# A second level of the seven-product scheme for three of 28 products per unit, with reordered copies, one buffer less for q, and a changed first unit and end

## The chip, the core and the metric

The kernel runs on one core of a Trainium2 chip. The metric is the device time of one execution in microseconds. A core has TensorE (PE, matrix products; its weight loads are listed apart as PEld), VectorE (DVE), ScalarE (ACT), GpSimd (POOL) and SyncE (SP, which here only issues DMAs). TensorE writes its results to PSUM, which has eight banks of 512 fp32 values per partition; the other engines' working memory is SBUF.

## What is computed

Attention over pooled keys and values, then a two-layer network with a sine in it. All numbers are fp32; q, k and v are 8 x 8 x 576 x 64 (batch, heads, sequence, head size), w_in is 512 x 2048, w_out is 2048 x 512.

```python
k_p = k.reshape(B, H, Sp, 8, D).mean(axis=3)          # Sp = 72
v_p = v.reshape(B, H, Sp, 8, D).mean(axis=3)
scores = scale * np.matmul(q, k_p.transpose(0, 1, 3, 2))
scores = scores - np.max(scores, axis=-1, keepdims=True)
attn = np.exp(scores)
attn = attn / (np.sum(attn, axis=-1, keepdims=True) + 1e-09)
x = np.matmul(attn, v_p)     # then heads are joined: 4608 tokens x 512
h = x @ w_in
s = np.sin(alpha * h)
g = h + s * s / (alpha + 1e-09)
out = g @ w_out
```

## The kernel before

**Two stages.** The first stage makes x batch by batch and g from it, and stores g to HBM ("g_bridge"). The second stage loads g and multiplies it by w_out. Line L796 is every matmul of x by w_in, L1133 every matmul of g by w_out.

**Seven products instead of eight.** Both stages use the scheme in which the product of two 2 x 2 block matrices takes seven block products, with sums of blocks made before and sums of products made after. In the first stage a block product is 256 features by 256 inputs by 256 tokens: two feature blocks and two input blocks of 128, so four matmuls with 256 moving columns. The sums of the weights are the tiles as1, as2, as4 (and a21, which is overwritten by a difference), the sums of x are in bt (tile "home3"). The second stage has applied the scheme twice all along (`outer` and `inner`), down to matmuls with 144 columns.

**Units, groups, slots.** The first stage runs over nine units of 512 tokens (`hidden(u, extra)`). A unit has four groups J of 2 x 256 features, and a group has seven slots k, one block product each, in the order 1, 5, 6, 2, 7, 3, 4. Slot numbers run from 0 to 27 within a unit, so that the third group (J = 2) begins at slot 14 and the fourth at slot 21. The whole program order on each engine is written out by hand. Before each slot's product, the list `self.left` of the slot before runs (the work on ScalarE and VectorE that belongs to the group: left0 to left6), then the list `extra[slot]`.

**Sums of products in PSUM.** The seven products accumulate in four banks, b1, b6, b5 and b7, taken in turn from banks 0 to 4. Product 1 goes to b1, and ScalarE copies b1 to b6; product 6 is added to b6, and ScalarE copies b6 to b7; product 5 goes to b5 and is copied to the SBUF tile p5. Products 2, 7, 3 and 4 are added to b1, b7, b6 and b7. The copies are L822 (b1 to b6), L836 (b6 to b7) and L838 (p5); VectorE's adds of p5 are L775. The sine is L802, the square L809, `finish` (L867) adds the squares to h, and `store_g` (L874) issues two DMAs from SP. h and g share the tile "h", which has two buffers.

**Attention in between.** While unit u runs, the attention of batch b = u + 1 is computed by `extra` work, placed by `carry(u)`: two_scores (L302) and its maxima and differences (two_shifts: L325, L326), exp (L351), norm (L357 to L359), turn (transposes on VectorE, L485 to L495), move (16 DMAs from SP, L505, tr to aM), all_values (L594 and L607 on TensorE, L521 to x on ScalarE). In all_values a copy of one column, named "order" (L601), stands between two parts of the matmuls into one bank. turn_q (L215, L218) transposes q of a later batch on VectorE, and 16 DMAs (L228) put it into place. Batch 0 is handled by first_batch, before unit 0. q tiles come from a pool with two buffers of one name; load_q is L80 and L101. load_v and load_k are followed by pooling sums on POOL (L127).

**The second stage.** `outputs()` runs 8 batches x 7 outer products; each has seven inner products, four matmuls each. For one outer product st, product 1 goes first and is copied to a second bank (L1230), and later products 6 and 7 each need a copy (L1253, L1272); in between stand products 5, 4, 2 and 3 of the outer product before it (`last`). `combine` adds the result to output blocks, `out` transposes a block on VectorE (L1155) and issues four DMAs (L1160).

Of the kernel before, what the change touches and what calls it, by code (L numbers as in the profile page):

```python
# [13 lines left out]
F32 = mybir.dt.float32  # L14
# [5 lines left out]
P = 128  # L20
# [20 lines left out]
class Kernel:  # L41
# [33 lines left out]
    def new_q(self, b):  # L75
        self.qm[b] = self.qp.tile([P, 5 * self.H * self.D], F32, name="q")
# [6 lines left out]
    def pairs_q(self, b, tiles):  # L83

        nc = self.nc
        if 0 in tiles:
            self.raw = self.q_views(self.qm[b])
            self.qm[b] = self.qp.tile([P, 5 * self.H * self.D], F32, name="q")
# [113 lines left out]
    def turn_q(self, b, part):  # L202
# [8 lines left out]
        if part == 0:  # L211
            for e in range(2):
                x = main[:, 4 * e:4 * e + 4].rearrange("p hp t (k i) -> p hp t k i", i=32).rearrange("p hp t k i -> p (hp t) k i")
                out = tr[:, :, 768 * e:768 * e + 512].rearrange("p k (n i) -> p n k i", i=32)
                nc.vector.transpose(out=out, in_=x)  # L215
            return
# [26 lines left out]
    def attention(self, b):  # L243
# [22 lines left out]
        def q_t(i, copy=nc.scalar.copy):  # L266
# [3 lines left out]
            if b not in self.qt:  # L270
                self.qt[b] = self.qt_view(self.qp.tile([P, 5 * H * D], F32, name="q"))
# [105 lines left out]
        def q_head(hp):  # L377

            if hp == 0:
                self.qt[b] = self.qt_view(self.qp.tile([P, 5 * H * D], F32, name="q"))  # L380
# [203 lines left out]
        def all_values():  # L584
# [16 lines left out]
            (nc.vector.tensor_copy if b > 1 else nc.scalar.copy)(out=self.sm.tile([P, 1], F32, name="order")[:], in_=rest[:, 1, 0:1])  # L601
# [6 lines left out]
            self.vp.pop(b)  # L608
            for hp in hps:
                to_x(ps[hp].rearrange("p (t j) -> p j t", t=4), hp, 0, 512)  # L610
# [149 lines left out]

    def sums_of_x(self, u, n):
# [9 lines left out]
    def hidden(self, u, extra):  # L771

        nc = self.nc
        bank = lambda: self.bank([P, JW, TH])
        add = lambda o, x, y: nc.vector.tensor_tensor(out=o, in0=x, in1=y, op=OP.add)  # L775

        for slot in range(7 * self.NJ):
            J, k = divmod(slot, 7)
            for f in self.left:
                f()  # L780
            for f in extra[slot]:
                f()
            if k == 0:
                before = self.group
                G = self.group = SimpleNamespace(
                    u=u, J=J, b1=bank(), g=self.hp.tile([P, 2, JW, 2, TH], F32, name="h"),
                    s=self.hp.tile([P, 2, JW, 2, TH], F32, name="s", bufs=1))
            xT, bt = self.xT[u], self.bt[u]
            B = lambda i, j: xT[:, 2 * i:2 * i + 2, j * TH:(j + 1) * TH]

            def product(p, ps, start):
                x = {1: B(0, 0), 2: B(1, 0), 3: B(1, 1), 4: bt[:, 3], 5: bt[:, 0], 6: bt[:, 1], 7: bt[:, 2]}[p]
                for jj in range(JW):
                    f = J * JW + jj
                    for kk in range(2):
                        nc.tensor.matmul(ps[:, jj, :], self.A[p][:, kk, f * P:(f + 1) * P], x[:, kk, :],  # L796
                                         start=(start and jj == 0 and kk == 0), stop=(kk == 1), skip_group_check=True)

            def sin(G, i, j, src):
                for jj in range(JW):  # L800
                    f = i * self.K2 // 2 + G.J * JW + jj
                    nc.scalar.activation(out=G.s[:, i, jj, j, :], in_=src[:, jj], func=AF.Sin, scale=self.al[:, f:f + 1])  # L802

            def square(G, i, js):

                for jj in range(JW):
                    f = i * self.K2 // 2 + G.J * JW + jj
                    x = G.s[:, i, jj, js, :]
                    nc.scalar.activation(out=x, in_=x, func=AF.Square, scale=self.c[:, f:f + 1])  # L809

            early = lambda G: G.J == (0 if G.u else 1)

            def squares(G):
                if not early(G):
                    square(G, 0, 1)
                square(G, 1, slice(0, 2))

            self.squares = squares

# [566 lines left out]
```

## Time and profile before

| | |
|---|---|
| three timed runs | 909.52, 909.93, 910.46 us |
| the profiled execution, span | 906.9 us |
| TensorE clock granted | 1.00 throughout |
| units 1 to 6 | 55.4 us each |
| first stage ends, second begins to dominate | about 519 us |
| last matmul ends | 901.8 us |
| ScalarE busy from 140 to 500 us | 257.10 of 360 us |
| VectorE busy from 140 to 500 us | 226.01 of 360 us |
| POOL busy from 140 to 500 us | 91.64 of 360 us |
| DMA engines' share and rate, 140 to 500 us | 0.60, 176 GB/s |

How to read it: a span is the time from the first to the last instruction that the profiler recorded, somewhat less than the device time. A busy share is an average over stages with different limits. An fp32 matmul appears as two records, each with its own weight load; the duration of a record (381 ns for 256 columns) is its latency, and since matmuls are pipelined the step from one to the next is shorter. In the groups, "idle before, releaser" tells how long the engine stood idle just before and what ended the wait. In the chain of waits each line is start, duration and what the chain ran through.

### The profile page before, as it was taken

To read this page: it belongs to the slowest core of one execution; us is meant where nothing else is said; L and a number is where in the kernel's file an instruction comes from. 1 tells how busy PE (TensorE), PEld (TensorE's weight loads), DVE (VectorE), ACT (ScalarE), POOL (GpSimd) and SP (SyncE) were. 2 spreads that over 40 slices of the span, in tenths; PEclk is the share of its full clock that TensorE was granted. 3 is DMA by queue.
4 is the path that set the end of the run, shared out by engine and by line. 5 is a ranking of instruction groups with operands and counts; after the bars stand their busy time and mean duration, and the time that the engine had idled before them with its cause. 6 is when DMAs were issued, how large, how long until landed. Compare 5 with 4: busy or idle time off the path is not lost.

```text
span 906.9 us, 17532 instructions
## 1 busy us (share of the span) xinstructions
PE 898.2 (99%) x6906; PEld 813.9 (90%) x6906; DVE 664.9 (73%) x1000; ACT 436.2 (48%) x998; POOL 169.9 (19%) x159
## 2 busy tenths in 40 slices
PE   8999999999999999999999999999999999999997
PEld 5787888888888788888888999999999999999997
DVE  7685766758467584664557799979798888889895
ACT  5696775867668676686976621111111111111111
POOL 4685340804408043130000000000000000000000
PEclk9999999999999999999999999999999999999999
DMA  9985867759567575548217247161618162534401
GB/s 263 243 250 157 220 172 191 191 169 251 174 167 184 168 195 173 143 128 308 77 69 244 96 132 214 43 207 40 223 27 229 35 194 68 171 92 131 131 15 40
DMA packets 128746, 141.12 MB, mean 156 GB/s; under 512 B 46920, under 2 KB 95704, under 8 KB 128664
## 3 DMA queue, kind: packets, MB, share of 16 engines
q1 hardware_dynamic: 126312, 137.99, 53.0%
q10 hardware_dynamic: 2352, 2.01, 0.8%
q8 instruction: 55, 0.90, 0.4%
q14 instruction: 27, 0.22, 0.1%
HBM read 75.37 MB, written 47.19 MB: 135 GB/s over the span
## 4 chain that ended last, share of the span: by engine, by line
PE 97%; DVE 1%; DMA 1%; ACT 1%; issue 0%; SPq 0%; DVEq 0%; ACTq 0%
PE PS L796 48%; PE PS L1133 42%; PE PS L302 2%; PE PS L594 2%; PE PS L607 1%; DMA h<-in_k_dram 1%; PE PS L406 0%; DVE h L867 0%; PE PS L552 0%; PE PS L263 0%; ACT s L809 0%; PE PS L199 0%; PE PS L550 0%; PE PS L460 0%; DMA out_dram<-o 0%
## 5 line engine op out<-in xcount | busy, mean ns | idle before, releaser
L796 PE MATMUL PS<-home,a 128*128 128x256 f32 x1152 | 264.4, 381 | 1.0 <-ACT home L521 0.5
L796 PEld LDWEIGHTS PS<-home,a 128*128 128x128 f32 x1152 | 216.5, 190 | 37.4 <-issue 5.0
L796 PE MATMUL PS<-home,as 128*128 128x256 f32 x864 | 200.0, 380 | 0.0
L796 PEld LDWEIGHTS PS<-home,as 128*128 128x128 f32 x864 | 162.6, 190 | 23.0 <-issue 0.8
L1133 PE MATMUL PS<-s,wb 128*128 128x144 f32 x896 | 119.4, 286 | 0.4 <-ACT PS L1253 0.4
L1133 PEld LDWEIGHTS PS<-s,wb 128*128 128x128 f32 x896 | 113.7, 190 | 0.7 <-ACT PS L1253 0.6
L809 ACT ACTIVATE s<-s,c 128x256 f32<-128x256 f32 (+1 forms) x216 | 110.0, 572 | 0.0
L127 POOL TENSOR_TENSOR kvin<-kvin 96x768 f32<-96x768 f32 (+3 forms) x42 | 72.5, 1726 | 197.6 <-DMA kvin<-in_v_dram 196.0
L775 DVE TENSOR_TENSOR h<-PS,p 128x512 f32<-128x512 f32 x72 | 49.1, 684 | 77.4 <-PE PS L796 44.6
L802 ACT ACTIVATE s<-h,al 128x256 f32<-128x256 f32 x144 | 65.1, 503 | 54.4 <-DVE h L775 53.8
L1253 ACT COPY PS<-PS 128x144 f32<-128x144 f32 x56 | 14.7, 263 | 146.3 <-PE PS L1133 142.0
L802 ACT ACTIVATE s<-PS,al 128x256 f32<-128x256 f32 x144 | 60.0, 467 | 32.8 <-PE PS L796 17.0
L1133 PE MATMUL PS<-s,a 128*128 128x144 f32 x512 | 73.2, 286 | 0.0
L1133 PE MATMUL PS<-r,wb 128*128 128x144 f32 x512 | 73.2, 286 | 0.0
L867 DVE TENSOR_TENSOR h<-PS,s 128x512 f32<-128x512 f32 x36 | 24.6, 684 | 62.4 <-ACT s L809 62.4
L1133 PEld LDWEIGHTS PS<-r,wb 128*128 128x128 f32 x512 | 67.1, 190 | 0.1
L1133 PEld LDWEIGHTS PS<-s,a 128*128 128x128 f32 x512 | 67.0, 190 | 0.0
L1272 ACT COPY PS<-PS 128x144 f32<-128x144 f32 x56 | 14.7, 263 | 88.2 <-PE PS L1133 88.2
L1133 PE MATMUL PS<-x,wb 128*128 128x144 f32 x384 | 54.9, 286 | 0.0
L1133 PE MATMUL PS<-s,we 128*128 128x144 f32 x384 | 54.9, 286 | 0.0
L1133 PEld LDWEIGHTS PS<-s,we 128*128 128x128 f32 x384 | 50.3, 190 | 0.1
L1133 PEld LDWEIGHTS PS<-x,wb 128*128 128x128 f32 x384 | 50.3, 190 | 0.0
(188 smaller groups left out, 1185.8 us busy)
## 6 DMA issues: line engine op xcount, KB each, us to landing
g_bridge<-h SPq DMA_DIRECT2D x72, 512.0 KB
r<-g_bridge SPq DMA_DIRECT2D x31, 1152.0 KB
out_dram<-o SPq DMA_DIRECT2D x124, 72.0 KB
kvin<-in_k_dram SPq DMA_DIRECT2D x14, 576.0 KB
q<-in_q_dram SPq DMA_DIRECT2D x7, 1024.0 KB
kvin<-in_v_dram SPq DMA_DIRECT2D x14, 512.0 KB
aM<-tr SPq DMA_DIRECT2D x54, 92.0 KB
aM<-tr SPq DMA_DIRECT2D x54, 88.0 KB
```

Source lines behind the costliest of these rows:

```text
L127: self.nc.gpsimd.tensor_tensor(out=t[..., 0:w] if w > D else out, in0=t[..., 0:w], in1=t[..., w:2 * w], op=OP.add)
L302: nc.tensor.matmul(ps[e][r0 + r:r0 + r + q.shape[-1], h, :], q[s], kb[s, hp, :], start=True, stop=True)
L594: nc.tensor.matmul(o[r:r + 64], w, x, start=start and i < 2, stop=False, skip_group_check=True)
L607: nc.tensor.matmul(ps[hp], w.rearrange("p e d -> p (e d)"), x, start=False, stop=True, skip_group_check=True)
L775: add = lambda o, x, y: nc.vector.tensor_tensor(out=o, in0=x, in1=y, op=OP.add)
L796: nc.tensor.matmul(ps[:, jj, :], self.A[p][:, kk, f * P:(f + 1) * P], x[:, kk, :], start=(start and jj == 0 and kk == 0), stop=(kk == 1), ...
L802: nc.scalar.activation(out=G.s[:, i, jj, j, :], in_=src[:, jj], func=AF.Sin, scale=self.al[:, f:f + 1])
L809: nc.scalar.activation(out=x, in_=x, func=AF.Square, scale=self.c[:, f:f + 1])
L867: add = lambda o, x, y: self.nc.vector.tensor_tensor(out=o, in0=x, in1=y, op=OP.add)
L1133: nc.tensor.matmul(out, W[:, J // 2, J % 2, :], A[:, J, :], start=(start and J == 0), stop=(J == self.NJ - 1), skip_group_check=True)
L1253: nc.scalar.copy(out=x1[:, 0, :], in_=x0[:, 1, :])
L1272: nc.scalar.copy(out=x1[:, 1, :], in_=x1[:, 0, :])
```

## The change

**Second level.** In units 1 to 6, product 5 of the third group and products 5 and 1 of the fourth group are not computed with four matmuls of 256 columns, but with the seven-product scheme once more: seven matmuls of 128 x 128 x 128. `inner_w_in` makes four sums of the weights per product, once, on POOL (slot 23 of unit 0); `inner_x` makes four sums of x per product and unit on POOL (slot 2). `inner_product` has four pieces: a (two matmuls into a spare bank, 7 or 6, and two ScalarE copies), b (two matmuls and a copy within the bank), d (one matmul and an add on VectorE) and e (two matmuls). The pieces are spread between the halves of the other products.

**Order in the third and fourth group.** The copies of the third group stand ahead of the last sines of the second group on ScalarE, and products 4, 6, 7 and 3 there are split in two or more parts. A part of `finish` and the store of the third group's g come later, in slots 23 and 25; `store_g` then stands behind the 16 DMAs of turn_q on SP's queue. The fourth group's first sine stands behind the "order" copy, which is now ScalarE's for all batches. The list `self.left` is gone; other groups keep their order. The tile s is allocated once for all groups.

**q.** One of the two q buffers now holds the weight sums from unit 0's slot 23 on, so that q of batch b = u + 2 is loaded at slot 7 of unit u instead of batch u + 3. For units from 1 on, the first two parts of turn_q move from slots 22 and 23 to 23 and 24. The second turn moves from slot 12 to 13.

**First unit and the second stage.** In unit 0 the last two_shifts moves from slot 11 to 12. In the second step of `outputs()` product 3 moves from before product 4 to behind product 6. At the end, one sum of output blocks goes to POOL, one block's transposes and DMAs are issued later, and the last DMAs are issued by SP and ScalarE in turn.

The core of the diff:

```diff
+    def inner_w_in(self):
+        w = self.q_tile(0)[:]
...
+            self.sums(((s1, L(1, 0), L(1, 1), OP.add), (s2, s1, L(0, 0), OP.subtract), (s3, L(0, 0), L(1, 0), OP.subtract), (s4, L(0, 1), s2, OP.subtract)))
+            self.W2[p] = J0, {1: L(0, 0), 2: L(0, 1), 3: s4, 4: L(1, 1), 5: s1, 6: s2, 7: s3}
...
+    def inner_x(self, u):
+        for p, x, out in ((5, self.bt[u][:, 0], self.last[:, 0:4 * P]),
+                          (1, self.xT[u][:, 0:2, 0:TH], self.ex[:, 5].rearrange("p h x -> p (h x)")[:, 0:4 * P])):
...
+    def inner_product(self, G, p, ps, y):
...
+        def a():
+            products((1, 5), (y[:, 0], y[:, 1]), True)
+            nc.scalar.copy(out=f[:, 0], in_=y[:, 0:1].to_broadcast([P, 2, P]))
+            m5[p] = self.sm.tile([P, 1, P], F32, name=f"m{p}", bufs=1)
+            nc.scalar.copy(out=m5[p][:], in_=y[:, 1:2])
+        def b():
+            products((6, 2), (c[1], c[0]))
+            nc.scalar.copy(out=c[2], in_=c[1])
+        def d():
+            products((7,), (c[2],))
...
+            nc.vector.tensor_tensor(out=f[:, :, 1], in0=x, in1=m5[p][:].to_broadcast([P, 2, P]), op=OP.add)
+        def e():
+            products((3, 4), (c[1], c[2]))
...
+            if k == 0:
...
+                if G.i5 and not N:
+                    G.i5.a()
+                if Q and not G.i5:
+                    self.last_sines(Q, 2)
+                extras()
+                if G.i1:
+                    G.i5.b()
+                    self.last_sines(Q, 0)
+                else:
+                    product(G, 1, G.b1, True)
+                    if G.i5:
+                        product(Q, 4, Q.b7, part=(2, 3))
+            elif k == 1:
+                if not G.i1:
+                    copy(G.b6[:], G.b1[:])
+                if G.i5 and not G.i1:
+                    self.last_sines(Q, 0)
...
+                elif G.i5:
+                    product(G, 6, G.b6, part=(0, 1))
+                    G.i5.b()
+                    self.last_sines(Q, 1)
+                    squares(Q, 0)
+                    product(G, 6, G.b6, part=(2, 3))
...
+                    self.finish(Q, (1,))
+                    self.store_g(Q)
...
-            (nc.vector.tensor_copy if b > 1 else nc.scalar.copy)(out=self.sm.tile([P, 1], F32, name="order")[:], in_=rest[:, 1, 0:1])
+            nc.scalar.copy(out=self.sm.tile([P, 1], F32, name="order")[:], in_=rest[:, 1, 0:1])
...
+            self.behind_order()
...
-            at(11, A.two_shifts)
+            at(12, A.two_shifts)
...
-            at(14, self.load_q, 3)
+            at(23, self.inner_w_in)
...
-                at((12, 12, 13, 13)[i], A.turn, i)
+                at((12, 13, 13, 13)[i], A.turn, i)
...
-            if u + 3 <= last:
-                at(7, self.load_q, u + 3)
+            if 2 < u + 2 <= last:
+                at(7, self.load_q, u + 2)
+            at(2, self.inner_x, u)
...
-                at(turn + part, self.turn_q, u + 2, part)
+                at(((turn, turn + 1) if u == 0 else (23, 24))[part] if part < 2 else turn + part, self.turn_q, u + 2, part)
...
-                out(st["u"], 0, 1, t, 5, queues=2 * (nc.sync, nc.scalar))
+                out(st["u"], 0, 1, t, 5, queues=both)
...
+                elif p == 5:
+                    nc.gpsimd.tensor_tensor(out=c["c"][:], in0=c["c"][:], in1=t[:], op=OP.add)
+                    add(c["a"][:], c["a"][:], t[:])
+                    later.append(lambda: out(u, 1, 1, c["a"], queues=both))
...
-                    out(u, 0, 1, t, 0, 5, (nc.sync, nc.scalar, nc.scalar, nc.scalar))
+                    out(u, 0, 1, t, 0, 5, both)
...
                 if k == 1:
-                    rest()
+                    second()
                 fourth()
...
                 if k != 1:
-                    rest()
+                    second()
+                third()
...
+            if later:
+                later.pop()()
...
-                self.qp = pool(att, "qp", 2)
+                self.qp = pool(att, "qp", 1)
```

## The prediction

> **What bounds the kernel now.** I read the page's busy shares first, then the chain of work that ended last, then the timelines of the engines round each place that the change touches. Page, busy shares and the chain's shares:
>
> ```profile
> PE 898.2 (99%) x6906; PEld 813.9 (90%) x6906; DVE 664.9 (73%) x1000; ACT 436.2 (48%) x998; POOL 169.9 (19%) x159
> ...
> PE 97%; DVE 1%; DMA 1%; ACT 1%; issue 0%; SPq 0%; DVEq 0%; ACTq 0%
> ```
>
> TensorE is busy for 898.2 of 906.9 us and is 97% of the chain. So time can go in two ways only: less matmul time, or fewer of its few gaps. And any new wait of TensorE is paid in full. The chain, in order of time:
>
> ```profile
> 10.45 0.59 PE PS L368 x4
> ...
> 15.29 0.87 PE PS L460 x8
> ...
> 53.80 0.69 DVE h L775
> 54.49 0.04 issue
> 54.53 8.90 PE PS L796 x40
> ...
> 244.33 2.33 PE PS L594 x43
> ...
> 265.19 34.78 PE PS L796 x160
> 299.96 3.02 PE PS L594 x42
> ...
> 525.93 0.27 ACT PS L1253
> 526.20 0.04 issue
> 526.25 370.72 PE PS L1133 x3024
> ```
>
> One fp32 matmul is two records. 34.78/160 is 217 ns for half a matmul of 256 columns, 370.72/3024 is 122.6 ns for one of 144. Line 265.19 also dates the slots of unit 4: 20 slots without a hole, 1.739 us each, so slot 14 begins at 280.84 and slot 25 at 299.97. Three spots show TensorE waiting: for VectorE's add L775 at 54.49, at L594 (3.02 us in unit 4, 2.33 in unit 3), for ScalarE's copy L1253 at 526.20. Next, how fast weights load (timeline of weight loads), then ScalarE and VectorE in unit 4:
>
> ```profile
> 8.61 0.53 PEld L368 LDWEIGHTS PS<-twos,home 128*128 128x128 f32 x4
> ```
> ```profile
> 280.21 0.90 ACT L802 ACTIVATE s<-h,al 128x256 f32<-128x256 f32 x2
> ...
> 283.23 0.59 ACT L822 COPY PS<-PS 128x512 f32<-128x512 f32 x1
> ...
> 294.82 0.57 ACT L822 COPY PS<-PS 128x512 f32<-128x512 f32 x1 [0.89 <-PE PS L796]
> ```
> ```profile
> 297.52 2.37 DVE L215 STREAM_TRANSPOSE tr<-q 128x1024 f32<-128x1024 f32 x2 [4.86 <-DMA aM<-tr]
> ...
> 302.14 0.12 DVE L601 COPY order<-PS 128x1 f32<-128x1 f32 x1
> ```
>
> At 283.23 ScalarE has no idle time in front: it is late in the third group. At 294.82 it waited for the product, and began 0.07 us after slot 22's start (294.75). At 302.14 the tiny "order" copy stands behind VectorE's transposes, which waited for a DMA: that is the 0.69 us of unit 4.
>
> **What the Trainium skill says.** "TensorE: Matmul & The Clock Gate", section "LDWEIGHTS (loading the stationary operand)": a load costs columns/1.2 ns, 107 for 128 columns, whatever the rows. The trace agrees: four loads in 0.53 us, the last 0.19 long (its mean), are (0.53 - 0.19)/3 = 113 ns apart beside moving blocks of 64. The same page, "Architectural detail: the array is 16× 32×32, not 1× 128×128": weight loads are pulled ahead, ScalarE and VectorE are strictly first in, first out. The trace's 217 ns with loads of 190 ns shows the overlap; so a late copy holds everything behind it. "DMA: Bandwidth & Descriptors", section "Issuing engines are not separate DMA queues": a second issuing engine saves issue time only, which is what the end needs.
>
> **The change part by part**, against the span of 906.9 us (the three timed runs have a median of 909.93; I carry the difference over).
>
> *Second level (product 5 of groups 2 and 3, product 1 of group 3, units 1 to 6: 18 products).* Removed: 4 matmuls of 256 columns, 8 x 217 = 1739 ns. Added: 7 of 128 columns, 14 records. Their step isn't in the trace with fp32 halves. Below: 109 ns (L460, 0.87/8, transposes of 128). Above: 122.6 (144 columns can't be quicker). I take 113, the load's own step: 1582 ns. Gain 157 ns each, 18 x 157 = 2.8 us; with the bounds 0.4 to 3.8.
>
> Each also adds three ScalarE copies (at most 0.38 + 0.26 + 0.26, from L1230 and L1253, whose blocks are larger), one VectorE add of 256 columns (0.45, L1088 of 288) and 128-column sums on POOL. POOL's eight sums per unit are about 0.46 us each (L127 of 128 columns), 3.7 us from slot 2, before the queue reaches load_v's wait at slot 6, and are needed at slot 14, 20 us later. The weight sums run once, at slot 23 of unit 0, from free POOL. All hidden, unless a hand-off is late. I walked unit 4's third and fourth group with these durations. ScalarE: after the sine at 280.21 the new copies take 281.0 to 281.6, then the copy of bank 1 can start when product 1 ends at 282.15 (+0.07), done 282.79; before it came at 283.23. Product 6 wants it at 283.02, since only half of product 4 (0.87 us) now lies between: 0.2 us to spare. The same 0.2 us recurs ahead of product 6 in the fourth group. The first copy for group 3's product 1 stands behind two squares pairs, a sine and a square and is done near 290.2; its matmuls come at 290.65: 0.4 to spare. VectorE's adds have 0.7 us or more. So no wait, but three margins below half a microsecond per unit. The copy, 0.57, plus both latencies, 0.07 and 0.04, must beat 0.87.
>
> *Order copy to ScalarE, half of the finish between the transposes, third transpose a slot later.* TensorE's L594 needs the copy about 2.05 us after the values start; ScalarE comes to it after two copies, 1.0 us after. Behind it stand a sine and the writes of x, not needed before the next unit. Unit 4's 0.69 us goes: 0.7. Zero in the other units (2.33). The DVE transposes, moved from slots 22 and 23 to 23 and 24, wait for the DMAs of aM anyway, until 297.5; turn's second piece moves behind the group's adds, total VectorE work the same.
>
> *SP's queue.* Third group's stores of g pass behind the 16 issues of q<-tr (0.63 us each, 10 us): issued near 312 instead of 301.6. Buffer h is wanted by the next unit's first group at about 318.7 (L775, one period of 55.4 us after 263.82). An estimate of the landing, 1 MB at 176 GB/s (the mean from 140 to 500 us), is 6 us: 318. Close, but the add may slip till product 4 of that group, 3 us later. Nothing. The load of q (one DMA of 1024 KB, two of 64 KB) leaves slot 14 of unit 0 and is issued at slot 7 of unit 1, and so on with one buffer: it passes moves and stores on SP, has 16 slots (28 us) till its transposes, and its buffer was released by the scores of slot 5 before too. Nothing; one megabyte less in the first 60 us, which helps nobody on the chain.
>
> *First unit.* The last shift leaves slot 11, so the add L775 is no longer behind 1.0 + 1.1 us of it: TensorE's gap of 0.45 us before 54.53 closes. The next add comes later for it, by some 0.1 us at ScalarE's next late copy (gap of 0.11 us at 63.43). 0.35.
>
> *Second stage's start.* The third product now lies between product 6 and 7, 0.98 us of matmuls over a copy of 0.27: the wait of 0.41 us at 526.25 goes. 0.4.
>
> *End.* Timeline:
>
> ```profile
> 899.81 4.70 SPq L1160 DMA_DIRECT2D out_dram<-o  x7
> ```
> ```profile
> 902.08 2.31 ACTq L1160 DMA_DIRECT2D out_dram<-o  x5
> ```
>
> Seven issues on SP, 0.67 us each, end at 904.51 and the program 2.4 us later; ScalarE has five, at 0.46. After: six and six, and one 0.72 us add leaves VectorE for idle POOL (about 1.3 us, L667's size; its reader, the add on "c", comes 1.6 us later). TensorE's last product, 900.71 + 0.98 + its drain, still sets the last add. Nothing before 902.9 improves; the last issue comes 0.6 us earlier. 0.6 (0 to 0.8).
>
> Sum: 2.8 + 0.7 + 0.35 + 0.4 + 0.6 = 4.9 us. 906.9 goes to 902.0, the median to 905.0. One part in 500 of the time, 1.8 us, is what a measurement of this kernel can tell from no change.
>
> **Rivals.**
>
> 1. *Margins half missed.* Each of six units loses 0.3 us at the two 0.2 us hand-offs. For it: the stream had 1.7 us there before, now 0.87. Against: latencies above are measured. 909.93 - 4.9 + 1.8 = 906.8.
> 2. *Weight loads bind.* Halves step at 122.6, the second level yields 0.4, and half of the small parts (2.05) hold: 909.93 - 1.4 = 908.5. For it: load and stream of 128 columns take the same time, no slack on either. Against: 109 to 113 in the trace.
> 3. *Slower: ScalarE late in the third group.* Place: the copy of bank 1 ahead of product 6, groups 2 and 3. If the sines and exponentials of group 1 run over (table loads of 1.28 us stand there) by 1.3 us more than in unit 4, each unit loses 1.3 us: 909.93 - 4.9 + 7.8 = 912.8. It decides from 0.8 us a unit. For it: no idle time before 283.23. Against: the new order puts that copy ahead of four activations, so that it needs only what precedes 281.1.
> 4. *That the change doesn't do what it says:* the programs' instruction order shows 14 records of 128x128 in place of 8 of 128x256 at 18 places, so no.
>
> **How the numbers follow.** Forecast 0.62, rival 1 0.17, rival 2 (no difference) 0.10, rival 3 0.11. Faster by over 0.2% (below 908.1): 0.62 + 0.17 = 0.79; same 0.10; slower 0.11. The forecast's own range, with the bounds 0.4/3.8 and 0/0.8: 903.8 to 908. For 8 in 10, down to 903.4 where small gaps elsewhere close too, up to 908.8, which takes in rivals 1 and 2.
>
> **What would show it.** The matmuls of 128 columns with a step near 113 ns and no idle time in front on TensorE; a unit of about 54.9 us against 55.4; 2.33 us at L594's counterpart in every unit; no gap at 54.5 and 526; SP's and ScalarE's last issues together by 904. Wrong would be: idle TensorE before product 6 of the third or fourth group, released by ScalarE's copy; steps near 122; an add of h waiting on the stores of g.

## The result, and the profile after

| | before | after |
|---|---|---|
| median of four timed runs beside each other | 909.72 us | 905.24 us |
| lowest, highest | 909.08, 910.46 | 904.48, 905.52 |
| span of the profiled execution | 906.9 us | 903.3 us |

The ratio is 0.9949, with a 95% interval of 0.9932 to 0.9966: faster by half a per cent, 4.5 us. The changed kernel was timed again later, on another chip, beside the kernel before: 905.16 against 909.36 us, 0.9953 (0.9940 to 0.9967).

To see where the time went I cut each trace at events of TensorE that both programs have: the first matmul of the seven products (L796 before, L834 after), the first matmul of each unit with 32 stationary columns in the values (L607 before, L613 after), the last matmul of the seven products, the end of the last matmul, the end of the span. Six pieces come out, in us:

| piece | before | after | gained | forecast |
|---|---|---|---|---|
| start, up to the first of the seven products | 19.93 | 20.46 | -0.53 | 0 |
| first unit, up to its values | 61.87 | 61.66 | 0.21 | 0.35 |
| the six periods from there | 332.01 | 329.02 | 2.99 | 2.8 + 0.7 |
| to the last matmul start of the first stage | 104.79 | 104.79 | 0.00 | 0 |
| second stage, to the end of the last matmul | 383.25 | 383.10 | 0.15 | 0.4 |
| end | 5.08 | 4.26 | 0.82 | 0.6 |
| span | 906.93 | 903.29 | 3.64 | 4.9 |

The start is the same work in both programs and varies between 19.86 and 20.46 us over all the profiled executions here. Without it, 4.17 us of the forecast 4.9 came.

Page of the changed kernel, busy shares and the shares of the chain:

```profile
PE 895.5 (99%) x7014; PEld 816.4 (90%) x7014; DVE 677.1 (75%) x1011; ACT 448.1 (50%) x1070; POOL 210.6 (23%) x216
...
PE 94%; DVE 2%; ACT 2%; DMA 1%; issue 0%; SPq 0%; DVEq 0%
```

TensorE has 108 records more (18 products, 14 records in place of 8) and still 2.7 us less busy time. It is still the bound, but 3% less of the chain runs over it: ScalarE and VectorE now stand in the chain at places where they did not. The chain of waits, in order of time (start, duration, what it ran through):

```profile
61.92 1.50 ACT ex L357 x2
...
64.04 8.87 PE PS L834 x40
...
279.71 3.52 PE PS L834 x16
...
298.74 2.33 PE PS L600 x43
...
535.61 2.48 DVE r L1265
538.13 360.92 PE PS L1310 x2944
```

At 298.74 unit 4's values take 2.33 us, as in all other units; before they took 3.02. The gap at 54.5 is gone, but the chain reaches the products at 64.04 over ScalarE's exponentials. The gap at 526 is gone, but at 538.13 the chain comes from a large sum on VectorE.

The second level itself, on the timeline of TensorE (start, duration of the group, engine, line, operands, count) in unit 4's third group:

```profile
282.14 1.09 PE L834 MATMUL PS<-home,as 128*128 128x256 f32 x4
283.07 0.39 PE L1014 MATMUL PS<-last,q 128*128 128x128 f32 x2
283.29 0.39 PE L1014 MATMUL PS<-home,as 128*128 128x128 f32 x2
283.51 1.03 PE L834 MATMUL PS<-home,as 128*128 128x256 f32 x4
```

The pair at 283.07 is followed by the pair at 283.29, which by the next at 283.51: 0.22 us for two records, so 110 ns each. The median step behind the 252 records of 128 columns is 111 ns; from one of them to the next the mean is 110.8 (109 to 112).

One line is longer than its twin: the four records at 282.14 take 1.09 us, those at 283.51 1.03. The timelines of weight loads and of ScalarE tell why:

```profile
281.50 0.41 PEld L834 LDWEIGHTS PS<-home,a 128*128 128x128 f32 x2
282.10 0.73 PEld L834 LDWEIGHTS PS<-home,as 128*128 128x128 f32 x4 [0.20 <-ACT PS L810]
```
```profile
280.48 0.26 ACT L1020 COPY m<-PS 128x128 f32<-128x128 f32 x1
281.48 0.57 ACT L810 COPY PS<-PS 128x512 f32<-128x512 f32 x1 [0.74 <-PE PS L834]
281.96 0.91 ACT L984 ACTIVATE s<-h,al 128x256 f32<-128x256 f32 x2
```

ScalarE is not late: it waited 0.74 us for product 1, and its copy of bank 1 ends at 282.05. The matmul that needs it was due at 282.14. But its weight load normally starts one record, 0.21 us, ahead (the pair at 281.50), and here it starts at 282.10, 0.20 us of idle time released by the copy. The first record begins on time and the second follows after 279 ns instead of 216. The same is seen in the fourth group, where the copy ends 0.108 us ahead and the step is 264 ns. Both are alike in all six units. Together that is 0.11 us per unit.

The end, from the timelines of the issuing queues, of POOL and of VectorE:

```profile
895.44 1.98 POOL L1360 TENSOR_TENSOR cc<-cc,cb 128x576 f32<-128x576 f32 x1 [501.59 <-DVE cb L1265]
...
896.99 3.90 SPq L1337 DMA_DIRECT2D out_dram<-o  x6
...
897.00 3.97 ACTq L1337 DMA_DIRECT2D out_dram<-o  x6
...
899.56 0.51 DVE L1332 STREAM_TRANSPOSE o<-cc 128x320 f32<-128x320 f32 x1
```

Both queues issue their last DMA by 900.97, 0.9 us after the last transpose; before, SP came 1.6 us after it (904.51 against 902.93).

### The profile page after: what moved, and what is told of

It is laid out like the page before. It is cut to its first block, busy times and chain, and to the rows that moved or that the text cites. A ratio compares the mean times of both kernels' runs of the same rounds, so it can differ in the third digit from the quotient of the medians.

```text
span 903.3 us, 17940 instructions
## 1 busy us (share of the span) xinstructions
PE 895.5 (99%) x7014; PEld 816.4 (90%) x7014; DVE 677.1 (75%) x1011; ACT 448.1 (50%) x1070; POOL 210.6 (23%) x216
## 4 chain that ended last, share of the span: by engine, by line
PE 94%; DVE 2%; ACT 2%; DMA 1%; issue 0%; SPq 0%; DVEq 0%
PE PS L834 44%; PE PS L1310 41%; PE PS L1014 3%; PE PS L308 2%; PE PS L600 2%; PE PS L613 1%; DMA h<-in_v_dram 1%; DVE x L1265 1%; DMA h<-in_k_dram 1%; ACT s L991 0%; DVE s L1265 0%; ACT ex L357 0%; DVE r L1265 0%; ACT s L984 0%; PE PS L558 0%; PE PS L269 0%
## 5 line engine op out<-in xcount | busy, mean ns | idle before, releaser
L834 PE MATMUL PS<-home,a 128*128 128x256 f32 x1104 | 257.8, 381 | 1.3 <-ACT PS L810 0.8
L834 PEld LDWEIGHTS PS<-home,a 128*128 128x128 f32 x1104 | 205.3, 190 | 34.3 <-issue 5.7
L834 PE MATMUL PS<-home,as 128*128 128x256 f32 x768 | 183.0, 382 | 0.0
L834 PEld LDWEIGHTS PS<-home,as 128*128 128x128 f32 x768 | 141.6, 190 | 19.8 <-ACT PS L810 1.2
L1360 POOL TENSOR_TENSOR cc<-cc,cb 128x576 f32<-128x576 f32 x1 | 2.0, 1980 | 501.6 <-DVE cb L1265 501.6
L991 ACT ACTIVATE s<-s,c 128x256 f32<-128x256 f32 (+1 forms) x228 | 113.5, 564 | 0.0
L810 ACT COPY PS<-PS 128x512 f32<-128x512 f32 x72 | 41.5, 576 | 34.9 <-PE PS L834 30.2
```

The lines of the kernel that those rows point to most:

```text
L810: copy = lambda o, x: nc.scalar.copy(out=o, in_=x)
L991: self.nc.scalar.activation(out=x, in_=x, func=AF.Square, scale=self.c[:, f:f + 1])
```

## The experiments

The theory (theory 1 in most expectations) is that of the prediction: 14 records at 111 ns in place of 8 at 216, hand-offs through ScalarE that nearly all hold, and small parts at the order copy, the second stage and the end. Rivals are that the gain lies in the rearrangement and not in the second level, that the margins are worth nothing, and that waits only move. All experiments start from the changed kernel. Where the time of one run is given, it decides nothing, since single runs of one kernel lie over 4 us apart (907.59 to 911.87 for the kernel before); there the trace is read. Traces are compared from the unit's first matmul where it matters, because the start varies by 0.6 us.

**Without the second level.** Products 5 and 1 go back to four matmuls of 256 columns, and the sums on POOL are gone. The order of copies, sines and split products in the third and fourth group hangs on the second level in the code and goes with it: in the six periods the order of the products on TensorE and of all work on ScalarE is that of the kernel before, but for the order copy. So the expectation's "the new order of copies" does not stay; the order copy on ScalarE, the q buffer, the first unit, the second stage and the end do.

```diff
-            if two and J > 1:
-                G.i5 = self.inner_product(G, 5, b5, 7)
-            if two and J == 3:
-                G.i1 = self.inner_product(G, 1, b1, 6)
...
-            at(23, self.inner_w_in)
...
-            at(2, self.inner_x, u)
```

> The changed kernel without its second level: every product has four matmuls of 256 columns again and the sums of weights and x on POOL are gone; the new order of copies, the order copy on ScalarE, the q buffer, the first unit and the end stay. Theory 1, the second level pays by fewer matmul columns: a unit returns from 55.06 to 55.44 us, six units give back 2.3 us, 907.5 us in all. Theory 2, the gain is from the moved copies and the edges and the second level is neutral: unit near 55.06, time near 905.2.

Measured: 908.26 us, ratio to the kernel before 0.9988 (0.9980 to 0.9996). The six periods take 332.00 us against 329.02, so taking the second level away costs 3.0 us there, 0.49 a unit (55.55 us against 55.06). Of this, 0.11 is not the matmuls': the values take 2.45 us in units 1 to 6, because in this order ScalarE reaches the order copy (302.22) behind a pair of sines and one of squares. The remaining 0.38 us agrees with the difference of 55.44 to 55.06 between the kernels before and after. The run alone does not part the second level from the order that comes with it. The steps do: in a period of 55.44 us before, 215 of the 220 steps from one record of 256 columns to the next are 215 or 216 ns, and the five others (three of 320, one of 244, one of 263) are there in the changed kernel as well. So there was no wait that a new order could have removed; what got shorter is the matmuls. Theory 1 holds: the second level is worth 2.3 us, a little over half of the 4.17.

**The second level and the order copy alone.** The first unit's shift, the second stage and the end are put back as they were.

```diff
-            at(12, A.two_shifts)
+            at(11, A.two_shifts)
...
                 if k == 1:
                     second()
+                    third()
                 fourth()
...
-                    out(u, 0, 1, t, 0, 5, both)
+                    out(u, 0, 1, t, 0, 5, (nc.sync, nc.scalar, nc.scalar, nc.scalar))
```

> The changed kernel with the first unit's shift, the third product of the second stage and the end put back as before; second level, q and order copy stay. Theory 1: units of 55.06 us, no unit with 3.02 us at the values, so 2.3 + 0.7 of the gain stays, 906.7 us. Theory 2: nearly nothing stays, 909 us or more.

Measured: 907.00 us, ratio 0.9967 (0.9955 to 0.9979). Units of 55.06 us and values of 2.33 us stay; the second stage takes 383.25 us and the end 5.09, both as before. So the small parts at the second stage and the end are worth 0.15 and 0.83 us. In the run without the second level they were there as well (383.10 and 4.32 us), so the two do not depend on each other.

**More work between the copy and product 6.** In the third group the first small matmuls of the second level (piece a) go from ahead of product 1 to behind the copy. In the fourth group two parts of product 4 stand behind the copy instead of one.

```diff
-                if G.i5 and not N:
-                    G.i5.a()
...
                     product(G, 1, G.b1, True)
                     if G.i5:
+                        copy(G.b6[:], G.b1[:])
+                        G.i5.a()
                         product(Q, 4, Q.b7, part=(2, 3))
...
-                    product(G, 4, G.b7, part=(1, 2))
+                    product(G, 4, G.b7, part=(1,))
                     N.i1.e()
                     copy(N.b6[:], N.b1[:])
                     extras()
-                    product(G, 4, G.b7, part=(3,))
+                    product(G, 4, G.b7, part=(2, 3))
```

> The changed kernel, with more TensorE work between the copy of bank 1 to bank 6 and product 6: in the third group piece a of the second level comes behind product 1 instead of ahead of it, in the fourth group two quarters of product 4 instead of one stand behind the copy. Theory 1, a weight load that can't start before the copy shows up as a long step: the two steps of 279 and 264 ns behind product 6's first record become 216, a unit loses 0.11 us, 54.95 us, 0.7 us in all, 904.6. Theory 2, the long steps belong to the change from 128 to 256 columns or to the bank: they stay, unit 55.06.

The same matmuls on the timeline of TensorE:

```profile
282.69 1.03 PE L834 MATMUL PS<-home,as 128*128 128x256 f32 x4
283.55 0.38 PE L1014 MATMUL PS<-last,q 128*128 128x128 f32 x2
```

1.03 us, no longer 1.09. No step of 279 or 264 ns is left in any of the six units, and five of the six periods are 0.09 to 0.11 us shorter than the changed kernel's (54.96 instead of 55.06, say). So the two long steps were the hand-offs, and they cost what they seemed to. The total does not show it: 905.95 us (0.9959, 0.9946 to 0.9971). In the profiled execution the first unit took 63.08 us, 1.4 more than in the changed kernel, with a second wait at 68.0. I come back to the first unit below.

**Less work between the copy and product 6.** In the third group the half of product 4 goes ahead of product 1, so that product 6 follows product 1 at once.

```diff
-                    product(G, 1, G.b1, True)
                     if G.i5:
                         product(Q, 4, Q.b7, part=(2, 3))
+                    product(G, 1, G.b1, True)
```

> The changed kernel with the half of product 4 that lies between product 1 and product 6 of the third group put ahead of product 1, so that nothing hides the copy. Theory 1, the rival of late copies as priced: TensorE idle for 0.07 + 0.57 + 0.04 = 0.68 us and up to 0.1 of weight load in each of six units, 55.06 + 0.7 = 55.75 us a unit, 909.6 us in all. Theory 2, the wait is made good elsewhere in the unit: under 55.4 us a unit.

Measured: 910.41 us, ratio 1.0010 (1.0003 to 1.0017); a unit takes 55.93 us. ScalarE and TensorE in unit 4:

```profile
284.68 0.57 ACT L810 COPY PS<-PS 128x512 f32<-128x512 f32 x1 [1.60 <-PE PS L834]
```
```profile
281.89 2.76 PE L834 MATMUL PS<-home,a 128*128 128x256 f32 x12
285.30 1.13 PE L834 MATMUL PS<-home,as 128*128 128x256 f32 x4 [0.66 <-ACT PS L810]
```

ScalarE again waits for the product. One half of a product, 0.87 us of matmuls, decides whether the change gains or loses. The loss is 0.87 us a unit, not the 0.7 expected, and this shows how a gap is to be read. The view says 0.66 us idle. The step from the last record before the gap to the first behind it is 1038 ns instead of 216, and the next step is 320 instead of 216 (279 in the changed kernel): 822 + 41 = 863 ns. The idle time as shown begins only at the end that the profile gives the record before, 379 ns after its start, while the stream would have gone on after 216. So a gap costs its idle time, plus about 0.16 us, plus about 0.1 for the first record behind it.

The hand-offs also tell how early the copy has to end. In the changed kernel it ends 0.093 and 0.108 us ahead of the matmul's start, and 63 and 48 ns are lost at the next step; here it ends 0.052 us ahead of the delayed start, and 104 are lost. Each time the two add up to 0.156 us (within 0.001), in all six units. In the run with more work in between the copy ends 0.54 us ahead, and nothing is lost. So an estimate from these 18 hand-offs is that a copy must end 0.16 us ahead of the matmul that adds to its bank.

**The order copy back on VectorE.** Only the engine of the small copy changes; the transposes' place and the split of `finish` stay.

```diff
-            nc.scalar.copy(out=self.sm.tile([P, 1], F32, name="order")[:], in_=rest[:, 1, 0:1])
+            (nc.vector.tensor_copy if b > 1 else nc.scalar.copy)(out=self.sm.tile([P, 1], F32, name="order")[:], in_=rest[:, 1, 0:1])
```

> The changed kernel with the order copy back on VectorE for batches from 2 on. Theory 1, in the kernel before only a VectorE that had waited for a DMA made the order copy late: with half of the finish moved between the transposes VectorE reaches it about 0.6 us earlier, so that the values take 2.33 us in nearly all units, at most 0.2 us more in one; the gain at this place comes from the order of VectorE's work as much as from the other engine. Theory 2, ScalarE is what removed the 0.69 us: at least one unit shows 2.6 us or more at the values.

VectorE in unit 4 of the kernel before, between the first transposes (297.52) and the order copy (302.14):

```profile
299.81 0.65 DVE L867 TENSOR_TENSOR h<-PS,s 128x512 f32<-128x512 f32 x1
300.39 1.20 DVE L867 TENSOR_TENSOR h<-h,s 128x1024 f32<-128x1024 f32 x1
301.51 0.70 DVE L218 STREAM_TRANSPOSE tr<-q 64x512 f32<-64x512 f32 x1
```

and in this experiment (in brackets: idle time before it, and what ended it):

```profile
297.44 1.23 DVE L219 STREAM_TRANSPOSE tr<-q 128x1024 f32<-128x1024 f32 x1
298.60 0.66 DVE L224 STREAM_TRANSPOSE tr<-q 64x512 f32<-64x512 f32 x1
299.48 0.16 DVE L607 COPY order<-PS 128x1 f32<-128x1 f32 x1 [0.21 <-PE PS L600]
299.55 1.21 DVE L1036 TENSOR_TENSOR h<-h,s 128x1024 f32<-128x1024 f32 x1
```

The copy waits for TensorE, not the other way round; the values take 2.33 us in every unit, and the time of the one run was 904.68 us (span 902.9). So in this order the engine of the copy is not what gained the 0.69 us; VectorE's queue ahead of it is. Two things changed there. Before, the transposes of q waited 21.9 us in all (six waits) for the DMAs of aM; in the changed kernel, and in this one, a single such wait of 1.7 us is left, since the transposes come a slot later. And before, both parts of `finish` (1.85 us) stood between the transposes and the copy; now the smaller one stands between the transposes, and the larger one, 1.21 us, behind the copy. They were not tried apart, but the traces tell which one counts. Counted from the first matmul of the values, the first transposes begin at -2.38 us in the slow unit before, at -3.2 to -3.7 in units 1, 2, 3 and 5, and at -2.56 here. So they are nearly as late as in the slow unit, and VectorE is free for the copy at 1.04 all the same. With the larger part of `finish` still ahead it would be free at 2.25 (an estimate, 1.04 + 1.21), where the slow unit had its copy at 2.24. In the run without the second level both parts are ahead again and VectorE is free at 2.26; there ScalarE's copy at 1.64 held the loss to 0.12 us.

**The exponentials of unit 0 later.** The wait of 0.81 us ahead of 64.04 stands behind a table load and two exponentials on ScalarE. Here these go from slot 15 to 17, so that they stand behind the copy; their norms and transposes move with them.

```diff
-                at((9, 9, 15, 15)[i], A.exp, i)
-                at((10, 10, 16, 16)[i], A.norm, i)
-                at((13, 13, 17, 19)[i], A.turn, i)
+                at((9, 9, 17, 17)[i], A.exp, i)
+                at((10, 10, 17, 17)[i], A.norm, i)
+                at((13, 13, 19, 19)[i], A.turn, i)
```

> The changed kernel with the exponentials of the last two pieces of the first unit's attention behind the copies of slot 17 (from slot 15), their norms in slot 17 and transposes in slot 19. Theory 1, TensorE's gap of 0.81 us at 63.4 us comes from ScalarE's copy of bank 6 standing behind a table load and two exponentials (2.8 us): the gap is below 0.1 us, and the first unit shorter by 0.3 to 0.8. Theory 2, the first unit is bound by POOL and what it waits for: the gap moves to VectorE's add of p5 at 67.5 us, and the first unit is as long as before.

```profile
64.99 1.89 PE L834 MATMUL PS<-home,as 128*128 128x256 f32 x8
67.72 2.64 PE L834 MATMUL PS<-home,a 128*128 128x256 f32 x11 [0.83 <-DVE h L809]
```

The wait at 64 is gone, and one of 0.83 us comes 3.7 us later, followed by two more, 0.78 us at 74.4 and 0.30 at 76.7. The first unit takes 63.43 us, 906.7 us in all: the wait moves and grows, as in theory 2. That POOL is what binds, as theory 2 had it, is not shown: the add of p5 that TensorE waits for at 67.72 runs at 67.01 in VectorE's queue, straight behind the sums over the very exponentials that were moved.

**One sum of the second stage on POOL.** To bring VectorE sooner to the sum that TensorE waits for at 538, one earlier small sum goes to POOL.

```diff
-            tt(s4, a(1, 2), s2, OP.subtract)
+            (nc.gpsimd if (u, n) == (0, 2) else nc.vector).tensor_tensor(out=s4, in0=a(1, 2), in1=s2, op=OP.subtract)
```

> The changed kernel with one of VectorE's sums of 128x576 of the second stage (the last one for the third product of batch 0) on POOL. Theory 1, of the 0.41 us that moving the third product frees, 0.26 was lost again at 538 us because VectorE had no idle time from 519 on: the gap of 0.26 us at 538 goes, and the stretch from the last first-stage matmul to the end of the last matmul is 382.85 instead of 383.10 us. Theory 2, the gap at 538 is something else: it stays.

The timelines of POOL and VectorE:

```profile
524.00 1.69 POOL L1305 TENSOR_TENSOR s<-r,s 128x576 f32<-128x576 f32 x1 [130.14 <-ACT ca L1353]
```
```profile
524.69 3.41 DVE L1265 TENSOR_TENSOR x<-r,r 128x2304 f32<-128x2304 f32 x1
```

The wait stayed, 0.33 us (906.82 us in the one run). VectorE saved a sum of 0.75 us and lost 0.86: the sum at 524.69 takes 3.41 us instead of 2.55, and POOL's runs beside its first 1.0 us. The Trainium skill, "Trainium Architecture — The Big Picture", section "What this means for kernel authors", says that VectorE and GpSimd share a pair of ports by an exclusive lock. The two numbers fit that: nearly the whole overlap was lost. So this run leaves open whether VectorE's queue sets the wait; the next one asks that.

**One transpose of the second stage later.** The block's transpose and its DMAs go behind the large sum of the next step.

```diff
-                out(u, 0, 0, o)
+                late.append(lambda: out(u, 0, 0, o))
...
                     outer(u, n)
+                if late:
+                    late.pop()()
```

> The transpose (and with it the output's DMAs) of the second product of each unit of the second stage is issued behind the large sum of the next step instead of ahead of it, so VectorE begins r<-r,r some 0.7 us earlier. Theory 1: the gap of 0.26 us ahead of the matmuls on r at 538.13 comes from VectorE's own queue, and is gone; the last product ends 0.26 us earlier. Theory 2: another wait (a buffer, a DMA) sets the sum's start; the gap stays at 0.2 to 0.3 us.

VectorE and TensorE of the changed kernel:

```profile
534.19 0.78 DVE L1332 STREAM_TRANSPOSE o<-cd 128x576 f32<-128x576 f32 x1
534.89 0.72 DVE L1265 TENSOR_TENSOR s<-x,s 128x576 f32<-128x576 f32 x1
535.52 2.55 DVE L1265 TENSOR_TENSOR r<-r,r 128x2304 f32<-128x2304 f32 x1
```
```profile
538.13 1.25 PE L1310 MATMUL PS<-r,wb 128*128 128x144 f32 x8 [0.26 <-DVE r L1265]
```

and of this one:

```profile
534.19 0.75 DVE L1265 TENSOR_TENSOR s<-x,s 128x576 f32<-128x576 f32 x1
534.86 2.55 DVE L1265 TENSOR_TENSOR r<-r,r 128x2304 f32<-128x2304 f32 x1
537.33 0.77 DVE L1332 STREAM_TRANSPOSE o<-cd 128x576 f32<-128x576 f32 x1
```
```profile
537.83 1.14 PE L1310 MATMUL PS<-r,wb 128*128 128x144 f32 x8
```

The wait is gone (1.14 us for eight records instead of 1.25, and no idle time ahead), and the second stage takes 382.58 us instead of 383.10, 0.52 less (904.77 us in the one run, where one of the six periods took 0.33 us more than in the changed kernel; why stays open). The gap had shown 0.26. By steps it was 543 - 123 = 0.42 and then 227 - 123 = 0.10, which is the 0.52: the same reading of a gap as above.

**The first unit's shift back in slot 11.**

```diff
-            at(12, A.two_shifts)
+            at(11, A.two_shifts)
```

> The changed kernel with the last shift of the first unit back in slot 11; nothing else differs. Looked at: the first unit, from the first matmul of the seven products to the first one of the values, 61.66 us in the changed kernel. Theory 1: the shift's place is worth the 0.35 us of the prediction; a gap of 0.45 to 0.8 us returns ahead of 54.5, the gap of 0.81 us ahead of 64.04 shrinks to 0.1, and the first unit takes 62.0 or more. Theory 2: the wait only changes its place, and the first unit takes 61.4 to 61.8.

The first unit took 61.37 us, 904.23 us in the one run. In eight profiled executions with the shift in slot 12 and the same instructions in that unit it took 61.53, 61.53, 61.53, 61.62, 61.66, 61.76, 62.08 and 63.08 us; with the shift in slot 11 this one, 61.87 (the kernel before) and 62.59 (the second level alone). The gap of 0.26 us at 54.27 came back and that at 64.04 shrank to 0.11. VectorE in the changed kernel:

```profile
52.98 0.69 DVE L809 TENSOR_TENSOR h<-PS,p 128x512 f32<-128x512 f32 x1 [0.86 <-ACT s L984]
53.59 1.05 DVE L331 TENSOR_REDUCE mx<-PS 128x12 f32<-128x864 f32 x1
54.74 1.06 DVE L332 TENSOR_TENSOR ex<-PS,mx 128x864 f32<-128x864 f32 x1
55.72 0.68 DVE L809 TENSOR_TENSOR h<-PS,p 128x512 f32<-128x512 f32 x1
```

and in this experiment:

```profile
52.56 1.06 DVE L332 TENSOR_TENSOR ex<-PS,mx 128x864 f32<-128x864 f32 x1
53.54 1.28 DVE L809 TENSOR_TENSOR h<-PS,p 128x512 f32<-128x512 f32 x2
```

ScalarE's copy of bank 6 and the matmuls that wait for it, in the changed kernel:

```profile
63.32 0.58 ACT L810 COPY PS<-PS 128x512 f32<-128x512 f32 x1
```
```profile
64.04 1.97 PE L834 MATMUL PS<-home,a 128*128 128x256 f32 x8 [0.81 <-ACT PS L810]
```

the copy in this experiment, and the copy and the earlier wait in the kernel before:

```profile
62.56 0.58 ACT L810 COPY PS<-PS 128x512 f32<-128x512 f32 x1
```
```profile
62.82 0.58 ACT L836 COPY PS<-PS 128x512 f32<-128x512 f32 x1
```
```profile
54.53 3.72 PE L796 MATMUL PS<-home,a 128*128 128x256 f32 x16 [0.45 <-DVE h L775]
```

The three traces begin the unit at 20.46, 19.86 and 19.93 us, so these times have to be counted from there. With the shift in slot 12, the first add comes ahead of the shift and TensorE's gap at 54.5 is gone; but the second add comes behind it, at 35.26 us of the unit instead of 34.28 here and 34.46 in the kernel before. ScalarE's sine waits 1.81 us for that add. In the other two ScalarE later stands idle for 0.55 us ahead of the copy of product 1, since it is ahead of TensorE; with the shift in slot 12 that idle time is gone. So ScalarE comes to the copy of bank 6 no earlier than before the change: at 42.87 us of the unit, against 42.89 in the kernel before and 42.70 here. TensorE, now without its gap, arrives earlier and waits: the products behind the copy begin at 43.59, 43.61 and 43.42. So the change turned two waits (0.45 and 0.11 us in the kernel before, 0.26 and 0.11 here) into one of 0.81. Theory 2.

**The two findings together.** The wider margins and the later transpose, beside the changed kernel again on the same chip.

> The two wider margins ahead of product 6 (as in wide) together with the later transpose (as in late_out). Theory 1: 0.1 us in each of six units and 0.26 us in the second stage, 0.8 to 0.9 us below the changed kernel on the same chip, near 904.3 where that has 905.2. Theory 2: the first unit's waits, which follow the start of the program, take it back; within 0.5 us of the changed kernel.

> The changed kernel as it is, on the chip of best: 905.2, ratio to the kernel before 0.995.

| | median of six | lowest, highest | ratio to before |
|---|---|---|---|
| changed kernel | 905.16 us | 904.40, 906.25 | 0.9953 (0.9940 to 0.9967) |
| with both | 904.18 us | 903.14, 905.56 | 0.9946 (0.9930 to 0.9961) |

In the traces the six periods take 328.39 us instead of 329.02 and the second stage 382.58 instead of 383.11, together 1.16 us less, and the first unit takes 61.53. The medians differ by 0.98 us, as theory 1 said, but the ranges of the runs overlap: the trace shows these gains, the times alone would not establish them.

## Why the prediction was right, and where not

The forecast was 905.0 us and the time 905.24. The likeliest case is the one that happened, but the sum was 0.7 us too large, and three of its terms did not come about as told. That the two medians lie within 0.3 us is in part luck: the gain of 4.5 us by the clock is less than the forecast 4.9, the traces show 4.17 without the start, and four runs of one kernel spread over 1.0 to 1.4 us.

*Second level, forecast 2.8 us, measured 2.3.* The step of 128 columns was taken as 113 ns, the load's own pace; it is 110.8. The Trainium skill, "TensorE: Matmul & The Clock Gate", section "LDWEIGHTS (loading the stationary operand)", gives 107 for the load alone, within 4% of it. By steps a unit gains 24 x 216 - 42 x 110.8 = 530 ns, more than the 471 of the forecast. But 0.11 us a unit is lost at the two hand-offs ahead of product 6 and some 0.04 at the changes between step lengths, and 0.385 is left, times six. The walk along ScalarE was right that no engine is late: the copy waits for product 1 in both cases. What failed is the statement "0.2 us to spare", in the step on the margins. Half of the 0.2 was never there. The slots were dated with 34.78/20 = 1.739 us, but that stretch holds the last record's own end; by the starts of the records a slot is 1.727, and slot 22 starts at 294.62, not at 294.75. So the copy at 294.82 had begun 0.20 us after the product's last step, not 0.07, and the changed kernel's begins 0.20 after it too (281.28 to 281.48). That left 0.09. Then the prediction set the end of the copy against the start of the matmul, and the one that waits first is the weight load, which the trace shows to start 0.21 us ahead of its matmul where nothing holds it. The same prediction had named that load ahead when it read the skill; it did not put it into the margin. The run with wider margins shows the 0.10 us, and the run without a margin shows what rival 3 would have looked like: slower than before.

*Order copy, forecast 0.7, measured 0.69.* The amount and the place were right. The reason was half right: that VectorE's queue held the copy holds, but ScalarE wasn't needed for it in the new order, as the run with the copy on VectorE shows. The reading of the line at 302.14 left out that both parts of `finish` stand between the transposes and the copy, and the larger one's place is what saves the time. The copy is also due sooner than 2.05 us after the values start: where it ended at 1.54 nothing was lost, where it ended at 1.79, in the run without the second level, 0.12 us was. The statement that the transposes "wait for the DMAs of aM anyway" is wrong: a slot later they hardly wait.

*First unit, forecast 0.35, measured 0.21 in one pair of traces.* This step failed. The wait at 54.53 went, and by steps it had cost 0.71 us (825 - 216 and 320 - 216). But the prediction gave 0.1 us to the add that now comes behind the shift. That add comes 0.8 us later in the unit and takes ScalarE's 0.56 us of idle time ahead of the copy of product 1, so that ScalarE's next late copy, of bank 6, comes at the same time in the unit as before. The wait for it grew from 0.11 to 0.81 us and took all of the gain back. With the shift put back, the first unit is not longer, so the move is worth nothing that these traces can show. What stays open is why the same instructions take between 61.53 and 63.08 us there; waits of 0.1 to 0.45 us between 67.5 and 68 come and go with it.

*Second stage, forecast 0.4, measured 0.15.* The wait at 526.25 went, as foreseen. It had cost more than the 0.41 shown, 694 - 123 = 0.57 and 227 - 123 = 0.10 by steps. A new wait at 538.13 cost 0.52 of it. The prediction looked only at the place that the moved product left, not at the next sum on VectorE, which TensorE now reached sooner.

*End, forecast 0.6, measured 0.82.* Just above its upper bound of 0.8; the run with the old end has 5.09 us there, those with the new one 4.26 to 4.35, apart from 5.70 in the run with a sum on POOL, whose issues took longer. POOL's add was taken as 1.3 us and took 1.98. Its reader waited 0.49 us for it, and this cost nothing because the add behind, at 899.07, waits for the last product in any case. What the sum on POOL, the later transposes and the even issues are worth one by one was not tried.

*SP's queue and q, forecast nothing.* The period of 104.79 us behind the six units and the values agree; nothing waited for a store of g.

*The rivals.* Rival 1 (0.3 us a unit lost at the hand-offs) has the right place and three times the size. Rival 2 falls with the step of 111 ns. Rival 3 falls, as ScalarE has 0.74 us of idle time ahead of the copy.

## What to carry to other kernels

A second level of the scheme turned 1.73 us of matmuls into 1.55 here, a gain so small that one missed hand-off eats it: a hand-off has to be done ahead of the matmul's start, here by 0.16 us, since the weight load waits for it too. A gap of TensorE costs more than its idle time in the view, here by about a quarter of a microsecond: compare steps. When a wait is removed, look for the next hand-off behind it, and ask whether the engine that serves it comes earlier too; in this kernel two removed waits came back there, one whole and one for the most part. And count times of two traces from the same event: here two units began 0.6 us apart, as much as the effects that were looked for.

## What the runs showed of the hardware that I had not expected

- A copy that ended 0.09 us ahead of the matmul that needs its bank still cost 63 ns, through the weight load that waited for it (279 ns to the next record instead of 216). In 18 such hand-offs the lead and the loss add up to 0.156 us.
- fp32 records of 128 x 128 weights and 128 columns follow at 111 ns, little more than half of the 216 of 256 columns, though each of their weight loads is recorded as 190 ns.
- An add of 128 x 576 on POOL took 1.98 us beside VectorE's work at the end and 1.69 us at 524; on VectorE it takes 0.75. Beside the latter a sum on VectorE went from 2.55 to 3.41 us, while the add and transpose of VectorE beside the former, 0.76 and 0.78 us, were as long as before. Of each pair the one that began second was the slow one: POOL's add of 1.98 us began 0.05 us behind VectorE's, and VectorE's sum of 3.41 us began 0.69 us behind POOL's.
